# A polysketch attention and feed-forward kernel on one core: the first chunk's preparation laid out and ordered anew

## The chip, the core and the metric

The kernel runs on one core of a Trainium2 chip. The core has a matrix engine (TensorE, PE in the profile, with its weight loads shown apart as PEld), a vector engine (VectorE, DVE), an activation engine (ScalarE, ACT), a general engine (GpSimd, POOL) and a queue engine (SyncE, SP) that issues most transfers. The five run their own instruction streams and wait for one another through semaphores. The metric is the time of the whole kernel on the device in microseconds (us), the median of several runs.

## The reference

Attention with a polynomial sketch in place of the softmax, for 4 batches, 4 heads, 1088 positions and head width 32, and then a feed-forward block of width 128 with a hidden width of 512 on the joined heads.

```python
def phi(x):                                    # r = 8, so 64 features
    a = np.einsum('rd,bhsd->bhsr', S1, x)
    b = np.einsum('rd,bhsd->bhsr', S2, x)
    return np.einsum('bhsi,bhsj->bhsij', a, b).reshape(*x.shape[:-1], r * r)
q_p, k_p = phi(q), phi(k)
kv = np.einsum('bhsf,bhsd->bhfd', k_p, v)
z = np.sum(k_p, axis=2)
attn = np.einsum('bhsf,bhfd->bhsd', q_p, kv) / (np.einsum('bhsf,bhf->bhs', q_p, z)[..., None] + 1e-06)
x = attn.transpose(0, 2, 1, 3).reshape(B, S, H * D)
xn = (x - mean(x)) / np.sqrt(var(x) + 1e-06) * g_ln
out = x + np.maximum(xn @ w_ch1, 0.0) @ w_ch2
```

The arrays q, k, v and g_ln are float32. The sketches S1, S2 and the weights w_ch1 (W1), w_ch2 (W2) are float64, and the kernel makes float32 of them itself.

## The kernel before

**Making floats.** A float64 arrives as two 32-bit words. The kernel takes the high word apart on VectorE (`split`: exponent bits in `ex`, mantissa bits in `bits`, a tensor_scalar each), makes the mantissa and the scaled exponent from them, adds the low word, and joins the parts: `floats(2)` gives the mantissa, `floats(3)` the low word, `floats(0)` and `floats(1)` the exponent on ACT (lines 225 to 235), or `exps` the exponent on POOL (237 to 243, two tensor_scalar); `add` (POOL, line 252) adds the low word; `signed` and `last` (VectorE, 184 and 260) put in the sign and exponent. W1 goes through this in two halves of 256 columns, W2 in one piece of 512. The sketches (128 x 64 numbers here, both sketches side by side, each row repeated for 16 groups of partitions) go through it in lines 188 to 202.

**Loads.** SP issues, in order: S2, the keys of batch 0 in two pieces (`kn`), its queries (`qn`), W1, its values in four pieces (`vn`), W2. ACT issues S1 and the vector g. Batch 0's values go on every fourth partition and its keys are turned into every fourth column; the other batches lie in blocks of 32. The loads of batch 1 and the keys of batch 2 are held back by one small copy on POOL (line 608) that writes into their first column after a piece of the features of the queries is there.

**Attention, batch by batch.** Keys are turned in 32 x 32 blocks by VectorE (`turn_k`, into `kT`), multiplied with the sketch (`key_features`, into `fs`), and multiplied pairwise into 64 features (`key_products`, on POOL and VectorE, into `kp`). `key_sums` and `key_scale` give the denominators' part that is put beside the sketch in `sq`; `key_values` and `key_spread` give the table `kvr`. Queries are turned (`turn_q`, into `qT`), multiplied with `sq` (`query_features`, PSUM tile X), turned back (`query_rows`, into `fq`), divided (`quotients`), multiplied pairwise (`query_products`) and turned (`query_turn`, into `qpT`). `numerators` multiplies `kvr` and `qpT`; `columns_of` copies the result to `xT`.

**Feed-forward, chunk by chunk.** A chunk is 512 rows; a batch gives two, and a last small one holds what is left of all four. `mean_free` multiplies W1 with a matrix that takes out the mean and holds g (`cg`), in two halves. `hidden` does one of four column blocks of W1 and the relu, `second` the product with W2 for 128 rows, `finish` scales and adds x. `turn_rows`, `stats` and `root` make the rows and their scales.

**Order.** Every engine runs its instructions in the order in which the kernel's text issues them; the order is written out by hand, lines 583 to 728 for batches 0 and 1, a loop from line 732 for the rest. `fill` issues matmuls of ones into a bank that nobody reads. What must be waited for is found from the tiles that instructions read and write. The first chunk is half prepared apart from the rest: `(0, 0, 4)` in the order means batch 0's first four of eight tiles of 32 columns.

Of the kernel before, what the change touches and what calls it, by code (L numbers as in the profile page):

```python
# [8 lines left out]
F32 = mybir.dt.float32  # L9
# [16 lines left out]
def kernel(  # L26
# [43 lines left out]
    XP = M[2]  # L70
# [6 lines left out]
    s_raw = const([P, 2 * D], S1.dtype, "s_raw")  # L77
    for eng, src, a in ((act, S1, 0), (nc.sync, S2, D)):
        eng.dma_start(out=s_raw[:, a : a + D],
                      in_=bass.AP(src.tensor, src.offset, [[0, P // R], [D, R], [1, D]]))  # L80
# [7 lines left out]
    act.dma_start(out=g_row, in_=moe_g_ln.rearrange("(o p) -> o p", o=1))  # L88
# [15 lines left out]
    def load_v(b):  # L104
        base = v.offset + b * H * S * D
        for r in range(4):
            n = SN[r] * D
            nc.sync.dma_start(
                out=_ap(vn[b], *((r, 32) if b == 0 else (32 * r, 32)), 0, [[VH, H], [1, n]],
                        step=4 if b == 0 else 1),  # L110
# [4 lines left out]
    for t in vn:  # L115
# [4 lines left out]
    nc.sync.dma_start(out=w1_raw, in_=moe_w_ch1)  # L120
    load_v(0)
    nc.sync.dma_start(
        out=w2_raw.rearrange("p (jc f) -> p jc f", f=DM),
        in_=moe_w_ch2.rearrange("(jc p) f -> p jc f", p=P),
    )
# [20 lines left out]
    dve.tensor_tensor(out=m8, in0=bit, in1=head, op=ALU.is_equal)  # L146
    kT = [const([P, NT * P], F32, f"kT{i}") for i in range(2)]
# [40 lines left out]
    s_f = const([P, 2 * D], F32, "s_f")  # L188
    if s_raw.dtype == F32:
        dve.tensor_copy(out=s_f, in_=s_raw)  # L190
    else:
        t = exponent(s_raw, P, 2 * D, "s")
# [10 lines left out]

    w1 = const([P, DH], F32, "w1")
# [5 lines left out]
    class weight:  # L210


        def __init__(self, dst, raw, tag):
            self.dst, self.raw, self.plain = dst, raw, raw.dtype == F32
            if not self.plain:
                self.t = exponent(raw, P, raw.shape[-1], tag)

        def cols(self, a, n):
            return {k: x[:, a : a + n] for k, x in self.t.items()}
# [17 lines left out]
        def exps(self, a=0, n=512):  # L237
            if not self.plain:
                t = self.cols(a, n)
                pool.tensor_scalar(out=t["exf"], in0=t["ex"], scalar1=-896.0, scalar2=0.0,  # L240
                                   op0=ALU.add, op1=ALU.max)
                pool.tensor_scalar(out=t["e2"], in0=t["exf"], scalar1=255.0, scalar2=2.0**23,
                                   op0=ALU.min, op1=ALU.mult)
# [18 lines left out]
    W1, W2 = weight(w1g, w1_raw, "w1"), weight(w2, w2_raw, "w2")  # L262


    def turn_k(b, r2):
        n = SN[r2]
        at, dims = (r2, [[1, 2], [P, n], [4, 32]]) if b == 0 else (
# [583 lines left out]
```

## Time and profile before

| what | value |
|---|---|
| median of 3 runs | 110.47 us (110.25 to 110.83) |
| the profiled execution: its time, its span | 110.73 us, 108.9 us |
| PE matmul busy | 100.2 us, 92% of the span |
| DVE, POOL, ACT busy | 70.9, 53.9, 39.2 us |
| moved by DMA | 14.19 MB, mean 130 GB/s |
| q of batch 0: issued, landed after | 2.78 us, 5.8 us |
| W1: issued, landed after | 3.26 us, 6.7 us |
| W2: issued, landed after | 6.39 us, 6.5 us |
| batch 1's loads: first issue | 13.67 us |
| first product of the feed-forward block | 19.31 us |

Times inside the profile count from the span's start. A busy PE is not PE at its peak, since matmuls are pipelined; a slice digit is a tenth of busy time. In a timeline row, "x4" is four instructions merged, and the bracket holds the time for which the engine stood idle before the row with the event that ended it. All that is changed runs in the first 26 us.

### The profile page before, as it was taken

The page shows a single profiled execution, that of the slowest core. Times are in us where ns is not written, and L with a number is a line of the kernel's source. Part 1 is how long each engine was busy: PE and PEld are TensorE (multiplying, and loading weights), DVE is VectorE, ACT ScalarE, POOL GpSimd, SP SyncE. Part 2 cuts the span into 40 slices and gives each one's busy share as a digit, 9 for nine tenths or more (in the row PEclk, how much of TensorE's full clock was granted, in tenths as well). Part 3 has the DMA queues.
Part 4 walks back from the last instruction along what each step waited for, and adds up shares of the span by engine and source line. Part 5 has one row for each costly group of instructions (what it writes and reads, how often), then busy time and mean ns, then how long its engine had stood idle before and what let it go on. Part 6 is the DMA issues. An engine that isn't in the chain of part 4 may idle for free. (4 is left out here: it accounts for less than half of the span.)

```text
span 108.9 us, 3605 instructions
## 1 busy us (share of the span) xinstructions
PE 100.2 (92%) x1496; PEld 67.3 (62%) x1496; DVE 70.9 (65%) x204; ACT 39.2 (36%) x79; POOL 53.9 (49%) x67
## 2 busy tenths in 40 slices
PE   6949996994999999999999999999999999999890
PEld 3317545445973677836963786559449658849680
DVE  5496989349859958789879703896950493274411
ACT  4103693662222532434316511451282251071220
POOL 7036682992997397672960693059340034016000
PEclk9999999999999999999999999999999999999998
DMA  1999159910002595334495862520036450132031
GB/s 24 251 332 360 62 174 341 264 45 3 6 0 102 155 303 149 143 106 124 82 355 181 204 211 76 152 56 17 3 76 219 122 163 11 48 91 53 0 96 48
DMA packets 12162, 14.19 MB, mean 130 GB/s; under 512 B 2417, under 2 KB 8946, under 8 KB 12146
## 3 DMA queue, kind: packets, MB, share of 16 engines
q1 hardware_dynamic: 11856, 13.87, 42.8%
q8 instruction: 11, 0.18, 0.7%
q10 hardware_dynamic: 290, 0.10, 0.3%
q14 instruction: 5, 0.04, 0.1%
HBM read 9.77 MB, written 4.19 MB: 128 GB/s over the span
## 5 line engine op out<-in xcount | busy, mean ns | idle before, releaser
L552 PEld LDWEIGHTS M<-w,hT 128*128 128x128 f32 x256 | 31.0, 191 | 7.7 <-issue 3.8
L552 PE MATMUL M<-w,hT 128*128 128x128 f32 x256 | 34.3, 281 | 1.5 <-DVE w L260 1.4
L542 PE MATMUL M<-xT,w 128*128 128x512 f32 (+1 forms) x72 | 34.2, 588 | 0.7 <-DVE ob L564 0.5
L544 ACT ACTIVATE hT<-M 128x512 f32<-128x512 f32 (+1 forms) x36 | 20.6, 574 | 33.7 <-PE M L542 33.7
L432 POOL TENSOR_TENSOR qp<-a,fq 128x1024 f32<-128x1024 f32 (+1 forms) x9 | 16.2, 1816 | 20.0 <-DVE a L425 20.0
L564 DVE SCALAR_TENSOR_TENSOR ob<-M,rstd,x 128x128 f32<-128x128 f32 x32 | 9.0, 344 | 16.5 <-PE M L552 7.1
L542 PEld LDWEIGHTS M<-xT,w 128*128 128x128 f32 x72 | 11.9, 189 | 9.9 <-issue 6.6
L330 POOL TENSOR_TENSOR kp<-fs 128x1024 f32<-128x1024 f32 (+2 forms) x8 | 16.2, 2036 | 2.2 <-ACT fs L324 1.4
L443 DVE STREAM_TRANSPOSE qpT<-qp 128x1024 f32<-128x1024 f32 (+1 forms) x10 | 10.8, 1082 | 4.0 <-POOL qp L432 3.9
L164 PE MATMUL M<-ones 128*128 128x512 f32 (+2 forms) x22 | 10.5, 591 | 1.1 <-DVE ones L86 1.1
L524 POOL TENSOR_SCALAR va<-mv 128x4 f32<-128x4 f32 (+1 forms) x9 | 2.1, 229 | 15.8 <-DVE mv L517 15.6
L526 POOL TENSOR_TENSOR rstd<-va,mhalf 128x4 f32<-128x4 f32 (+1 forms) x9 | 9.0, 1000 | 0.7
L461 PE MATMUL X<-qpT,kvr 32*32 32x256 f32 (+2 forms) x384 | 7.5, 323 | 1.0 <-DVE qpT L443 1.0
L515 DVE BATCH_NORM_STATS2 st<-x 128x6 f32<-128x128 f32 x34 | 7.4, 279 | 0.3
L461 PEld LDWEIGHTS X<-qpT,kvr 32*32 32x32 f32 x384 | 4.5, 103 | 4.4 <-ACT loww L235 1.8
L269 DVE STREAM_TRANSPOSE kT<-kn 128x576 f32<-128x576 f32 (+1 forms) x8 | 6.4, 822 | 1.0 <-DMA kn<-in_k_dram 1.0
L476 ACT COPY xT<-X 128x512 f32<-128x512 f32 (+1 forms) x8 | 4.2, 561 | 7.7 <-PE X L461 7.7
L164 PEld LDWEIGHTS M<-ones 128*128 128x128 f32 x22 | 4.4, 226 | 4.1 <-issue 2.7
L409 DVE STREAM_TRANSPOSE fq<-X 128x512 f32<-128x512 f32 (+1 forms) x9 | 5.8, 669 | 1.0 <-PE X L399 1.0
L507 DVE STREAM_TRANSPOSE x<-xx 128x512 f32<-128x512 f32 (+1 forms) x8 | 5.4, 669 | 0.8 <-DMA xx<-xd 0.8
L358 PEld LDWEIGHTS FB<-kp,vn 128*32 128x32 f32 x288 | 4.2, 110 | 2.6 <-POOL kp L330 1.5
L387 DVE STREAM_TRANSPOSE qT<-qn 128x1024 f32<-128x1024 f32 (+1 forms) x5 | 5.1, 1015 | 0.6 <-DMA qn<-in_q_dram 0.6
(100 smaller groups left out, 85.5 us busy)
## 6 DMA issues: line engine op xcount, KB each, us to landing
qn<-in_q_dram SPq DMA_DIRECT2D x4, 544.0 KB, 5.5
out_dram<-ob SPq DMA_DIRECT2D x33, 64.0 KB, 1.8
xd<-xT SPq DMA_DIRECT2D x7, 256.0 KB, 2.6
xx<-xd SPq DMA_DIRECT2D x28, 64.0 KB, 2.0
kn<-in_k_dram SPq DMA_DIRECT2D x3, 544.0 KB, 6.3
vn<-in_v_dram SPq DMA_DIRECT2D x8, 144.0 KB, 5.1
w_raw<-in_moe_w_ch_dram SPq DMA_DIRECT2D x2, 512.0 KB, 6.6
vn<-in_v_dram SPq DMA_DIRECT2D x8, 128.0 KB, 5.8
```

Source lines behind the costliest of these rows:

```text
L164: pe.matmul(bank[:, 0:w], ones, _ap(ones, 0, P, 0, [[0, w // P], [1, P]]), start=True, stop=True)
L269: dve.transpose(_ap(kT[b % 2], 0, P, at, dims), _ap(kn[b], 0, P, D * ST[r2], [[D * n, 2], [D, n], [1, D]]),)
L330: eng.tensor_tensor(out=_ap(o, 0, P, H * F * t0, [[F, (t1 - t0) * H], [R, R], [1, R]]), in0=_ap(a, 0, P, at, [[R, (t1 - t0) * H], [1, R], ...
L432: eng.tensor_tensor(out=_ap(qp[p, t0 // 4], 0, P, H * F * (t0 % 4), [[F, m], [R, R], [1, R]]), in0=_ap(a2s[p], 0, P, HR * t0, [[R, m], [1, ...
L443: dve.transpose(_ap(qpT[p], 0, P, 32 * t0, [[32, n], [width(p), 8], [1, 32]]), qp[p, t0 // 4][:, o : o + n * H * F],)
L461: pe.matmul(X[D * h : D * h + D, 512 * r + 32 * t0 : 512 * r + 32 * (t0 + n)], kvr[p if p < 4 else r][rows, DM * i + D * h : DM * i + D * ...
L515: dve.bn_stats(out=st[:, 6 * t : 6 * t + 6], in_=x[c][:, P * t : P * (t + 1)])
L526: pool.tensor_tensor(out=rs[:, 0:n], in0=va[:, 0:n], in1=mhalf[:, 0:n], op=ALU.pow)
L542: pe.matmul(hp[:, 0:n], w1[:, P * j : P * (j + 1)], xT[c][:, 0:n], start=True, stop=True)
L544: act.activation(_ap(hT[c], 0, P, 512 * j, dims), hp[:, 0:n], AF.Relu)
L552: pe.matmul(po[c][:, DM * t : DM * (t + 1)], hT[c][:, 512 * j + P * t : 512 * j + P * (t + 1)], w2[:, DM * j : DM * (j + 1)], start=(j == ...
L564: dve.scalar_tensor_tensor(out=ob[c][:, P * t : P * (t + 1)], in0=po[c][:, P * t : P * (t + 1)], scalar=rstd[c][:, t : t + 1], in1=x[c][:, ...
```

## The change

- The sketches are loaded on every fourth partition, S1 on partitions 0, 4, 8, ..., S2 on 1, 5, 9, ..., into a 128 x 32 tile that POOL clears first. After one transpose both lie in one 32-column tile. For the copy of S2 spread over heads (`sketches2`), a matmul with a 0/1 matrix `pick` (from an iota on POOL and a comparison on VectorE) brings its rows to all groups in PSUM.
- Batch 0's keys and values have the same layout as the other batches; `turn_k` can do a range of tiles, and batch 0's keys are turned in four pieces, after the sketches.
- g, W1 and W2 are issued by ACT, after its step for the sketches' mantissa.
- W1's first half is split into PSUM (bank M[0]), its second half later into SBUF.
- W2's exponents are computed by VectorE instead of POOL.
- `kn[1]`'s first column, which holds back the loads of batch 1, is written by ACT from the quotients' result, after `key_spread`.
- The order up to chunk 0's third hidden product is new; the fills go to X, and there are fewer of them. The copy of W1's first finished half moves from ACT to VectorE; the clearing of a part of kT[0] is gone.

```diff
--- before.py
+++ after.py
@@ -67,17 +67,18 @@
 
     X = ps.tile([P, 2048], F32, name="X")
     M = [ps.tile([P, 512], F32, name=f"M{i}") for i in range(3)]
-    XP = M[2]
     FB = ps.tile([P, 512], F32, name="FB")
 
     def const(shape, dtype, name):
         return consts.tile(shape, dtype, name=name)
 
 
-    s_raw = const([P, 2 * D], S1.dtype, "s_raw")
-    for eng, src, a in ((act, S1, 0), (nc.sync, S2, D)):
-        eng.dma_start(out=s_raw[:, a : a + D],
-                      in_=bass.AP(src.tensor, src.offset, [[0, P // R], [D, R], [1, D]]))
+
+    s_raw = const([P, D], S1.dtype, "s_raw")
+    pool.memset(s_raw.bitcast(U32), 0)
+    for eng, src, a in ((act, S1, 0), (nc.sync, S2, 1)):
+        eng.dma_start(out=_ap(s_raw, a, H * R, 0, [[1, D]], step=4),
+                      in_=bass.AP(src.tensor, src.offset, [[0, H], [D, R], [1, D]]))
     one = const([P, 1], F32, "one")
     dve.memset(one, 1.0)
     warm = const([P, 1], F32, "warm")
@@ -85,7 +86,6 @@
     ones = const([P, P], F32, "ones")
     dve.memset(ones, 1.0)
     g_row = const([1, P], moe_g_ln.dtype, "g_row")
-    act.dma_start(out=g_row, in_=moe_g_ln.rearrange("(o p) -> o p", o=1))
     kn = [const([P, G * D], F32, f"kn{b}") for b in range(B - 1)]
     kn.append(kn[0])
     qn = [const([P, G * D], F32, f"qn{b}") for b in range(B)]
@@ -106,8 +106,7 @@
         for r in range(4):
             n = SN[r] * D
             nc.sync.dma_start(
-                out=_ap(vn[b], *((r, 32) if b == 0 else (32 * r, 32)), 0, [[VH, H], [1, n]],
-                        step=4 if b == 0 else 1),
+                out=_ap(vn[b], 32 * r, 32, 0, [[VH, H], [1, n]]),
                 in_=bass.AP(v.tensor, base + ST[r] * D, [[G * D, 32], [S * D, H], [1, n]]),
             )
 
@@ -117,12 +116,7 @@
     load_rows(kn, k, 0, 0, 18)
     load_rows(kn, k, 0, 18, G)
     load_rows(qn, q, 0)
-    nc.sync.dma_start(out=w1_raw, in_=moe_w_ch1)
     load_v(0)
-    nc.sync.dma_start(
-        out=w2_raw.rearrange("p (jc f) -> p jc f", f=DM),
-        in_=moe_w_ch2.rearrange("(jc p) f -> p jc f", p=P),
-    )
 
 
     top = const([P, 1], F32, "top")
@@ -144,6 +138,9 @@
     dve.tensor_scalar(out=bit, in0=row, scalar1=3, scalar2=3,
                       op0=ALU.logical_shift_right, op1=ALU.bitwise_and)
     dve.tensor_tensor(out=m8, in0=bit, in1=head, op=ALU.is_equal)
+    pick = const([P, P], F32, "pick")
+    away = const([P, P], I32, "away")
+    pool.iota(away, [[0, P // R], [4, R]], base=1, channel_multiplier=-1)
     kT = [const([P, NT * P], F32, f"kT{i}") for i in range(2)]
     for t in kT:
         pool.memset(t[:, 8 * P :], 0.0)
@@ -185,11 +182,11 @@
                                  op0=ALU.bitwise_and, op1=ALU.bitwise_or)
 
 
-    s_f = const([P, 2 * D], F32, "s_f")
+    s_f = const([P, D], F32, "s_f")
     if s_raw.dtype == F32:
         dve.tensor_copy(out=s_f, in_=s_raw)
     else:
-        t = exponent(s_raw, P, 2 * D, "s")
+        t = exponent(s_raw, P, D, "s")
         split(t)
         act.activation(t["mant"], t["bits"], AF.Identity, bias=one, scale=2.0**-20)
         dve.tensor_scalar(out=t["exf"], in0=t["ex"], scalar1=-896.0, scalar2=0.0,
@@ -201,6 +198,13 @@
                                  op0=ALU.mult, op1=ALU.add)
         dve.tensor_tensor(out=s_f, in0=t["mant"], in1=t["e3"].bitcast(F32), op=ALU.mult)
 
+    act.dma_start(out=g_row, in_=moe_g_ln.rearrange("(o p) -> o p", o=1))
+    act.dma_start(out=w1_raw, in_=moe_w_ch1)
+    act.dma_start(
+        out=w2_raw.rearrange("p (jc f) -> p jc f", f=DM),
+        in_=moe_w_ch2.rearrange("(jc p) f -> p jc f", p=P),
+    )
+
     w1 = const([P, DH], F32, "w1")
     w2 = const([P, JC * DM], F32, "w2")
     w1g = const([P, DH], F32, "w1g")
@@ -210,13 +214,19 @@
     class weight:
 
 
-        def __init__(self, dst, raw, tag):
+        def __init__(self, dst, raw, tag, bank=None):
             self.dst, self.raw, self.plain = dst, raw, raw.dtype == F32
+            self.bank = bank
             if not self.plain:
                 self.t = exponent(raw, P, raw.shape[-1], tag)
 
         def cols(self, a, n):
-            return {k: x[:, a : a + n] for k, x in self.t.items()}
+            t = {k: x[:, a : a + n] for k, x in self.t.items()}
+            if self.bank is not None and a == 0:
+
+                y = self.bank.bitcast(U32)
+                t["ex"], t["bits"] = y[:, 0:n], y[:, n : 2 * n]
+            return t
 
         def split(self, a=0, n=512):
             if not self.plain:
@@ -237,10 +247,10 @@
         def exps(self, a=0, n=512):
             if not self.plain:
                 t = self.cols(a, n)
-                pool.tensor_scalar(out=t["exf"], in0=t["ex"], scalar1=-896.0, scalar2=0.0,
-                                   op0=ALU.add, op1=ALU.max)
-                pool.tensor_scalar(out=t["e2"], in0=t["exf"], scalar1=255.0, scalar2=2.0**23,
-                                   op0=ALU.min, op1=ALU.mult)
+                dve.tensor_scalar(out=t["exf"], in0=t["ex"], scalar1=-896.0, scalar2=0.0,
+                                  op0=ALU.add, op1=ALU.max)
+                dve.tensor_scalar(out=t["e2"], in0=t["exf"], scalar1=255.0, scalar2=2.0**23,
+                                  op0=ALU.min, op1=ALU.mult)
 
         def signed(self, a=0, n=512):
             if not self.plain:
@@ -259,16 +269,15 @@
                 t = self.cols(a, n)
                 eng.tensor_tensor(out=dst, in0=t["mant"], in1=t["e3"].bitcast(F32), op=ALU.mult)
 
-    W1, W2 = weight(w1g, w1_raw, "w1"), weight(w2, w2_raw, "w2")
-
-
-    def turn_k(b, r2):
-        n = SN[r2]
-        at, dims = (r2, [[1, 2], [P, n], [4, 32]]) if b == 0 else (
-            32 * r2, [[32, 2], [P, n], [1, 32]])
+    W1 = weight(w1g, w1_raw, "w1", bank=M[0])
+    W2 = weight(w2, w2_raw, "w2")
+
+
+    def turn_k(b, r2, t0=0, t1=NT):
+        n = min(t1, SN[r2]) - t0
         dve.transpose(
-            _ap(kT[b % 2], 0, P, at, dims),
-            _ap(kn[b], 0, P, D * ST[r2], [[D * n, 2], [D, n], [1, D]]),
+            _ap(kT[b % 2], 0, P, 32 * r2 + P * t0, [[32, 2], [P, n], [1, 32]]),
+            _ap(kn[b], 0, P, D * (ST[r2] + t0), [[D * SN[r2], 2], [D, n], [1, D]]),
         )
 
     HR, W = H * R, H * R2
@@ -278,23 +287,25 @@
 
     def sketches():
 
-        s_t = const([P, W], F32, "s_t")
+        s_t = const([P, 32], F32, "s_t")
         dve.transpose(s_t, s_f)
         dve.tensor_tensor(
             out=_ap(sk, 0, P, 0, [[HR, 2], [R, H], [1, R]]),
-            in0=_ap(s_t, 0, P, 0, [[HR, 2], [R, H], [1, R]]),
+            in0=_ap(s_t, 0, P, 0, [[1, 2], [0, H], [4, R]]),
             in1=_ap(m32, 0, P, 0, [[0, 2], [1, H], [0, R]]),
             op=ALU.mult,
         )
         for b in range(B):
             pool.tensor_copy(out=_ap(sq[b], 0, P, 0, [[R, 2], [1, R]]),
-                             in_=_ap(s_t, 0, P, 0, [[HR, 2], [1, R]]))
+                             in_=_ap(s_t, 0, P, 0, [[1, 2], [4, R]]))
+        dve.tensor_scalar(out=pick, in0=away, scalar1=0, scalar2=None, op0=ALU.is_equal)
 
     def sketches2():
 
+        pe.matmul(FB[:, P : P + D], pick, s_f, start=True, stop=True)
         dve.tensor_tensor(
             out=_ap(s2b, 0, P, 0, [[D, H], [1, D]]),
-            in0=_ap(s_f, 0, P, D, [[0, H], [1, D]]),
+            in0=_ap(FB, 0, P, P, [[0, H], [1, D]]),
             in1=_ap(m8, 0, P, 0, [[1, H], [0, D]]),
             op=ALU.mult,
         )
@@ -580,84 +591,84 @@
     def mean_free(a, bank):
         pe.matmul(bank[:, 0:half], cg, w1g[:, a : a + half], start=True, stop=True)
 
-    fill(2, XP, 512)
-    turn_k(0, 0)
+    fill(2, X, 512)
     sketches()
-    turn_k(0, 2)
-    fill(1, XP, 512)
+    turn_k(0, 0, 0, 4)
+    turn_k(0, 2, 0, 4)
+    turn_k(0, 0, 4)
+    turn_k(0, 2, 4)
+    fill(1, X, 256)
+    key_features(0, 0, 4, M[0])
+    key_products(pool, 0, 0, 4)
+    key_features(0, 4, 9, M[1])
+    turn_q(0, 0, 4)
     pe.matmul(FB[:, 64:65], g_row, one[0:1], start=True, stop=True)
+    sketches2()
     act.copy(g_col, FB[:, 64:65])
-    pool.tensor_scalar(out=cg, in0=ident, scalar1=-1.0 / DM, scalar2=g_col,
-                       op0=ALU.add, op1=ALU.mult)
-    sketches2()
-    key_features(0, 0, 4, M[0])
-    key_features(0, 4, 9, M[1])
-    key_products(pool, 0, 0, 4)
-    turn_q(0, 0, 4)
-    fill(1, XP, 256)
+    fill(1, X)
     key_sums(0, FB, 0)
-    fill(1, XP)
+    fill(1, X)
     key_scale(0, FB, 32)
     key_products(pool, 0, 4, 6)
     key_products(dve, 0, 6, 9, M[1], 4)
-    fill(1, XP)
+    W1.split(0, half)
+    fill(1, X)
     query_features(0, 0, 4)
-    W1.split()
+    W1.floats(3, 0, half)
     query_rows(0, 0, 4)
-
-    pool.tensor_copy(out=kn[1][:, 0:1], in_=fq[0][:, 0:1])
+    for step in (2, 0, 1):
+        W1.floats(step, 0, half)
+    pool.tensor_scalar(out=cg, in0=ident, scalar1=-1.0 / DM, scalar2=g_col,
+                       op0=ALU.add, op1=ALU.mult)
+    quotients(0, 0, 4)
+    key_values(0)
+    key_rows()
+    W1.floats(3, half, half)
+    fill(1, X, 256)
+    key_spread(0, M[1], 0)
+
+    act.copy(kn[1][:, 0:1], a2s[0][:, 0:1])
     load_rows(kn, k, 1)
     load_rows(qn, q, 1)
     load_v(1)
     load_rows(kn, k, 2)
-    W1.floats(3)
-    W1.floats(2, 0, half)
-    W1.add(0, half)
-    W1.floats(0, 0, half)
-    W1.floats(1, 0, half)
-    W1.floats(0, half, half)
-    quotients(0, 0, 4)
-    fill(1, XP, 512)
-    fill(1, XP, 256)
-    key_values(0)
-    key_rows()
-    W1.floats(1, half, half)
-    fill(1, XP, 256)
-    key_spread(0, M[0], 0)
     query_products(0, pool, 2, 2)
     query_products(0, dve, 0, 2)
     query_turn(0, 0, 2)
     query_turn(0, 2, 2)
+    W1.add(0, half)
     W1.signed(0, half)
     W1.last(dve, 0, half)
-    W1.floats(2, half, half)
-    W1.add(half, half)
+    W1.split(half, half)
     W2.floats(3)
-    fill(1, XP, 512)
+    fill(1, X, 512)
+    fill(1, X, 256)
     numerators(0, 0, 4)
     columns_of(0)
+    for step in (0, 1, 2):
+        W1.floats(step, half, half)
     mean_free(0, M[0])
-    act.copy(w1[:, 0:half], M[0][:, 0:half])
+    dve.tensor_copy(out=w1[:, 0:half], in_=M[0][:, 0:half])
+    turn_q(0, 4, 4)
+    W1.add(half, half)
+    W2.split()
     W1.signed(half, half)
     W1.last(dve, half, half)
-    W2.split()
     W2.exps()
-    turn_q(0, 4, 4)
+    fill(1, M[2])
+
+
+    hidden(0, 0)
     W2.floats(2)
-    fill(1, XP)
-
-
-    pool.memset(kT[0][:, 8 * P + 64 :], 0.0)
-    hidden(0, 0)
     W2.add()
-    mean_free(half, FB)
-    act.copy(w1[:, half:], FB[:, 0:half])
     query_features(0, 4, 4)
     hidden(0, 1)
     W2.signed()
     query_rows(0, 4, 4)
     turn_k(1, 0)
     W2.last(dve)
+    mean_free(half, FB)
+    act.copy(w1[:, half:], FB[:, 0:half])
     turn_rows(0)
     hidden(0, 2)
     quotients(0, 4, 4)
```

## The prediction

> **What bounds the kernel now.** I read the page's busy table and slices first, then the list of waits, then the order of instructions in time from 0 to 32 us, where all the edits lie. The slices put TensorE (PE) near 9 tenths almost everywhere except at the start; the digit of the tenth slice (24.5 to 27.2 us) holds a real gap.
>
> ```profile
> PE   6949996994999999999999999999999999999890
> POOL 7036682992997397672960693059340034016000
> DMA  1999159910002595334495862520036450132031
> ```
>
> After about 26 us PE hardly rests, so time taken out of the start should come out of the end, and time put in should stay in. The chain that ended last covers only the final 6 us and says nothing of the start; so I follow the start's two visible stalls in the order of time. Columns are start, duration, engine, line, operation, and in brackets the idle time before it with its releaser.
>
> ```profile
> 8.63 0.71 DVE L387 STREAM_TRANSPOSE qT<-qn 128x512 f32<-128x512 f32 x1 [0.57 <-DMA qn<-in_q_dram]
> 9.19 3.17 POOL L330 TENSOR_TENSOR kp<-fs 128x1024 f32<-128x1024 f32 x2 [1.36 <-ACT fs L324]
> 9.77 0.96 DVE L330 TENSOR_TENSOR kp<-M,fs 128x768 f32<-128x768 f32 x1 [0.43 <-ACT fs L324]
> 10.65 0.78 DVE L178 TENSOR_SCALAR exw<-w_raw 128x512 uint32<-128x512 uint32 x1
> 11.34 1.30 DVE L180 TENSOR_SCALAR bitsw<-w_raw 128x512 uint32<-128x512 uint32 x1
> 12.56 0.70 DVE L409 STREAM_TRANSPOSE fq<-X 128x512 f32<-128x512 f32 x1
> 14.69 1.58 POOL L432 TENSOR_TENSOR qp<-a,fq 128x512 f32<-128x512 f32 x1 [0.36 <-DVE a L425]
> 16.31 0.71 DVE L443 STREAM_TRANSPOSE qpT<-qp 128x512 f32<-128x512 f32 x1 [0.22 <-POOL qp L432]
> ...
> 18.57 0.42 DVE L178 TENSOR_SCALAR exw<-w_raw 128x512 uint32<-128x512 uint32 x1
> 18.90 0.42 DVE L180 TENSOR_SCALAR bitsw<-w_raw 128x512 uint32<-128x512 uint32 x1
> ```
>
> VectorE (DVE) is the thread here: it waits for q of batch 0, and its two splits of W1 take 0.78 and 1.30 us, though the same shapes take 0.42 each at 18.57, where POOL is idle. POOL's two key products end near 11.15 (9.19 plus 1.96 for the 1024-wide form) and at 12.36 (9.19 + 3.17), and the two splits end just after these instants, 11.43 and 12.64: each got through only when a POOL product had ended. I call the end of the second product transpose T: 16.31 + 0.71 = 17.02. The numerators, the first hidden product (19.31) and all that follows hang on it.
>
> ```profile
> 19.07 2.05 POOL L240 TENSOR_SCALAR exfw<-exw 128x512 f32<-128x512 uint32 x1 [2.12 <-DVE exw L178]
> 21.20 1.94 POOL L242 TENSOR_SCALAR e2w<-exfw 128x512 uint32<-128x512 f32 x1
> 23.18 0.69 DVE L184 SCALAR_TENSOR_TENSOR e3w<-w_raw,e2w 128x512 uint32<-128x512 uint32 x1 [3.24 <-POOL e2w L242]
> 23.31 1.69 POOL L252 TENSOR_TENSOR mantw<-mantw,loww 128x512 f32<-128x512 f32 x1
> 25.09 0.65 DVE L260 TENSOR_TENSOR w<-mantw,e3w 128x512 f32<-128x512 f32 x1
> 25.88 2.02 PE L552 MATMUL M<-w,hT 128*128 128x128 f32 x16 [1.36 <-DVE w L260]
> ```
>
> Second stall: W2's exponents hold POOL 4 us, DVE idles 3.24 us, and PE stands 1.36 us before the second product at 25.88, which is T + 8.86. The question is how far that instant moves.
>
> **Start, to q's transpose.** The new memset of s_raw (about 0.1 to 0.2 us, from POOL's 128-wide memsets at 0.21) goes ahead of both sketch loads, and on SP's queue ahead of k and q: 0 to 0.2 us later; the sketch loads are a quarter as large, which may give that back. Keys: the two transposes with stride took 1.20 and 1.07; the plain forms took 0.73 (24.43) and 0.70 (26.80). In four pieces, with about 0.15 fixed each (0.70 for 512 columns, 1.25 for 1024), that is 1.43 + 2 x 0.15 = 1.75. They begin at 5.44, or at 6.0 for the later half of k (issued 2.31, landed in 3.7), so key features can start near 6.9 rather than 8.00. This removes the 0.43 us wait for fs at 9.77, but not the wait for q, so alone it buys no more than 0.43. Iota, the pick mask and its matmul lie under the wait for q; the copy of S2 now reads PSUM after that wait and costs DVE 0.27 (row L295).
>
> The queue: g, W1 and W2 are issued by ACT after its s mantissa (3.47 + 0.35), near 3.9, 4.6 and 5.3 at 0.65 to 0.72 each; ACT is otherwise idle until its first fs copy, so the issue is free. In the kernel before, W1 stands behind q on SP; now it runs beside q. q landed at 8.58. Lower bound of the delay 0, upper 1.5 (512 KB of W1 at the 350 GB/s of those slices all passing ahead of q's last pieces). I take 0, since q was issued near 2.8, about 2 us ahead of W1.
> The Trainium skill, DMA: Bandwidth & Descriptors, section "Issuing engines are not separate DMA queues", says that transfers from different engines share the same 16 DMA engines and interleave, which speaks against any gain from ACT's queue and for a later q; by the rule alone q would be up to that upper bound later and the sum 0.8 slower than before instead of 0.7 faster, and no run here shows two queues side by side yet.
> v of batch 0 gets 0.4 us earlier in issue and loses some bandwidth; key values need it only near 11 to 12.9, with slack.
>
> **From q to T.** DVE's order becomes: query transpose 0.71, S2 0.27, key product 0.96, half split of W1 into PSUM, feature transpose 0.70, quotients 1.31 (13.30 to 14.61), POOL's query product 1.66 (14.61 to 16.27), last transpose 0.75 (16.27 to 17.02). No row has DVE write such a split to PSUM. Bounds for two 256-wide pieces: 0.4 (half of two free 0.42 rows) and 2.08 (if they still queue behind POOL). I take 0.7: 256 columns at the 0.96 us per 768 of the key product, which touches PSUM and ran freely beside POOL. Sum 0.71 + 0.27 + 0.96 + 0.70 + 0.70 + 1.31 + 1.66 + 0.75 = 7.06 against 17.02 - 8.63 = 8.39: T comes 1.33 earlier. At the upper bound, which is the case that PSUM does not do what it is named for, the sum is 8.44, nothing is gained here, and the whole change is about 0.7 slower (111.2); against it stands the key product at 9.77, with one operand in PSUM, unhindered at 0.96.
>
> ACT's W1 steps (0.37 to 0.51 each) fall between; the three of the first half end by about 13, before kvr needs ACT. Fills removed before key values were 1.56 us of PE from 11.63; nothing then waited for key values but kvr (15.68), so no gain. The first-half mean_free keeps its place: numerators, then 0.70, then a copy of 0.37, now on DVE; hidden stays at T + 2.29.
>
> **From T to the second product.** DVE: W1's first half 0.85 under the numerators, half split, copy (to T + 2.24), query transpose 0.70, W2's splits 0.75, giving T + 3.6 with overlaps. POOL's add of W1's second half waits for ACT's three steps after the xT copy, T + 1.83 + 1.51 = T + 3.34. It takes 0.73. DVE's signed and last (0.85) follow; then POOL's W2 add, which took 1.69 including some 0.56 under DVE's L184 (23.31 to 23.87), so 1.13 alone. DVE's new exponents: two 512-wide, 0.75 as the splits; then signed to last 2.56 (23.18 to 25.74). If DVE and POOL exclude one another as at 10.65, both adds lie in DVE's thread: 3.6 + 0.73 + 0.85 + 1.13 + 0.75 + 2.56 = 9.62, less some 0.3 of overlaps at the handovers, plus 0.14 to the matmul: T + 9.5, which is 0.64 worse than 8.86. If they do not, 9.5 - 1.86 = 7.64, and PE's own work (19.31 to 24.51, 5.2, from T + 2.29, plus about 0.4 for the later w1 copy) sets T + 7.9, 0.96 better. I take the first, the nearest rows. POOL's 4 us leave, but were not worth 4: the new owner is the busier engine.
>
> **The gate of batch 1.** Its copy moves to ACT behind kvr, about 14.3 to 15 rather than 13.33, so six loads go up to 1.5 us later on SP, and behind it ACT's W2 low words. k of batch 1 landed in 4 to 8 us and is wanted at 24.43, q at 30.64: covered; without the cover each late us would count in full.
>
> **Sum.** 1.33 - 0.64 = 0.69 earlier. The profiled execution took 110.73 (span 108.9, 1.83 around it): 110.04. The median of the runs, 110.47, is 0.26 lower; from it 109.8.
>
> **Rivals.**
> 1. The locks overlap little (chance 0.22): 1.33 + 0.96 = 2.3 earlier, 108.2. For it: transposes at 23.79 and 24.43 ran normally under POOL's add. Against: the adds become ready during split and exponents, not transposes.
> 2. Slower (0.22): q lands late. Place: the query transpose at 8.63. Price: 1.5 less the 0.69, so 0.8 slower, 111.3. It decides from a start later than 9.3, where no gain is left. For it: the DMA digits are at 9 from 2.7 us wherever q is in flight. Against: q's head start.
> 3. PE runs at its slow rate (0.14): the opening fills shrink from six 512-wide passes (1.07 to 6.23) to four and two narrow ones, near 5.35. In the trace those passes follow 0.86 apart and later ones 0.43. Key sums, key scale and query features hold 0.38 + 0.25 + 0.51 of PE between q and DVE's feature transpose (rows at 9.83, 10.55 and 11.19); doubled, and with the key features late as well, 0.3 to 1 reaches DVE: about 110.4, no change.
> The Trainium skill, TensorE: Matmul & The Clock Gate, Part 1, gives about 3.4 us of activity for full rate, on a free-running window; the trace's 5.2 us of passes at half rate agree with no fixed delay of 3.4 us, and by the page alone 4.3 us of fills would suffice and this rival would fall away.
> The forecast keeps 0.42.
>
> **Numbers.** Half a per cent, 0.55 us, is about what a measurement of this kernel can tell from no change. Faster (below 109.92): 0.27 from the forecast, all of rival 1, 0.05 of rival 3: 0.54. Within: 0.13 + 0.06 + 0.06 = 0.25. Slower: 0.02 + 0.16 + 0.03 = 0.21. The time is 109.8; its own range 109.2 to 110.4. The wider range, 107.9 to 111.2, takes in rival 1 with 0.3 around it and rival 2 up to just short of its full price; about 0.05 is left out below and 0.13 above.
>
> **What would show it.** Splits of W1 at about 0.35 each beside POOL's products; T near 15.7; POOL's W2 add lying inside DVE's exponent stretch, with a DVE exponent row of 1 us or more; second product near 25.2 with PE still waiting for w. Wrong if the query transpose starts after 9.3, if W1's second half holds mean_free, or if the gain at 25 us isn't the gain at the end.

## The result and the profile after

The changed kernel takes 114.06 us (median of 4 runs, 113.58 to 114.55) against 110.65 for the kernel before in the same comparison: a ratio of 1.0321, 95% interval 1.0257 to 1.0385. It is 3% slower where 0.7 us less was forecast. The ratios here leave out executions that took over 1.5% more than the fastest of their kernel, so a ratio can differ a little from that of two medians, and three of the profiles below are of such executions (their times stand beside them).

The profiled execution took 114.02 us, its span is 112.2 us (108.9 before), its mean granted clock 0.966 (0.996). The slices of the page, 2.8 us each:

```profile
PE   6994299898699999999999999999999999999890
POOL 7347052061299567684692198019612025007000
PEclk9999755999999999999999999999999999999998
DMA  0889701996000279152387474440026440122031
```

The gap that PE had in the tenth slice is there as before, now in the eleventh (digit 6). A new hole stands in the fourth and fifth slices (8.4 to 14 us), and the clock line, all nines before, falls to 7, 5, 5 in the fifth to seventh. The timeline of the changed kernel shows what fills these slices (columns as in the prediction):

```profile
8.79 0.71 DVE L398 STREAM_TRANSPOSE qT<-qn 128x512 f32<-128x512 f32 x1 [2.13 <-DMA qn<-in_q_dram]
...
12.45 0.43 DVE L175 TENSOR_SCALAR M<-w_raw 128x256 uint32<-128x256 uint32 x1 [1.90 <-DMA w_raw<-in_moe_w_ch_dram]
12.91 0.43 DVE L177 TENSOR_SCALAR M<-w_raw 128x256 uint32<-128x256 uint32 x1
13.24 0.70 DVE L420 STREAM_TRANSPOSE fq<-X 128x512 f32<-128x512 f32 x1
13.91 2.15 PE L369 MATMUL FB<-kp,vn 128*32 128x64 f32 x72 [2.07 <-DMA vn<-in_v_dram]
...
16.98 0.71 DVE L454 STREAM_TRANSPOSE qpT<-qp 128x512 f32<-128x512 f32 x1 [0.22 <-POOL qp L443]
17.44 2.33 PE L161 MATMUL X<-ones 128*128 128x512 f32 x4
17.68 0.37 ACT L385 COPY kvr<-M 128x256 f32<-128x256 f32 x1 [0.85 <-PE M L384]
19.70 1.07 PE L472 MATMUL X<-qpT,kvr 32*32 32x128 f32 x64
22.00 1.10 PE L553 MATMUL M<-xT,w 128*128 128x512 f32 x2 [0.39 <-DVE w L651]
...
24.42 1.28 POOL L262 TENSOR_TENSOR mantw<-mantw,loww 128x512 f32<-128x512 f32 x1 [0.71 <-ACT mantw L243]
24.44 1.54 DVE L250 TENSOR_SCALAR exfw<-exw 128x512 f32<-128x512 uint32 x1
26.01 0.43 DVE L252 TENSOR_SCALAR e2w<-exfw 128x512 uint32<-128x512 f32 x1
...
29.17 2.02 PE L563 MATMUL M<-w,hT 128*128 128x128 f32 x16 [1.45 <-DVE w L270]
```

The same steps of PE and ACT in the kernel before:

```profile
13.12 1.21 PE L358 MATMUL FB<-kp,vn 128*32 128x64 f32 x72
15.31 0.37 ACT L374 COPY kvr<-M 128x256 f32<-128x256 f32 x1
17.17 1.06 PE L461 MATMUL X<-qpT,kvr 32*32 32x128 f32 x64 [1.04 <-DVE qpT L443]
```

Reading down: q is on time (8.79 against 8.63 before). After its key product DVE has the split of W1 next in its stream and stands 1.90 us on W1's load; the feature transpose behind it starts at 13.24 instead of 12.56. PE waits 2.07 us for batch 0's values. Windows of half a us show the granted clock at 1.00 until 12.0, 0.86 to 12.5, 0.50 from there to 19.0, 0.81 to 19.5. At half clock the key values take 2.15 (1.21 before), and from their start to the end of the copy to `kvr` it is 18.05 - 13.91 = 4.14 (15.68 - 13.12 = 2.56 before). The fill of 768 columns ahead of the numerators takes 2.33 and ends after the data are ready: T is 16.98 + 0.71 = 17.69 and `kvr` is there at 18.05, but the numerators start at 19.70, T + 2.0. Before, they started at 17.17, T + 0.15. From the first hidden product to the second product it is 29.17 - 22.00 = 7.17 (25.88 - 19.31 = 6.57 before). The second product comes 3.29 later than before, and the span is 3.3 longer.

Of the 3.29, 2.53 are there when the numerators start (19.70 against 17.17), and two loads and the clock are in them; 0.60 come between the first hidden product and the second product, where the forecast had 0.64. The windows of 1 us, kernel before and then changed kernel (columns: window, its length, PE busy with its matmuls, granted clock, DMA share, GB/s):

```profile
9.00:10.00 1.00, 1.00 (x29) 1.00 1.06 365
10.00:11.00 1.00, 1.00 (x30) 1.00 1.00 334
11.00:12.00 1.00, 1.00 (x35) 1.00 0.36 119
```

```profile
9.00:10.00 1.00, 0.08 (x8) 1.00 1.09 251
10.00:11.00 1.00, 1.00 (x29) 1.00 1.06 245
11.00:12.00 1.00, 0.83 (x34) 1.00 1.11 196
12.00:13.00 1.00, 0.00 (x0) 0.68 0.87 223
```

The DMA engines are as fully occupied (share about 1) at some 0.7 of the bytes per us (251 against 365, 245 against 334), and a stream that thins out from 11 us on before goes on past 13.

### The profile page after: what moved, and what is told of

The parts are those of the page before. It is cut to its first block, busy times and chain, and to the rows that moved or that the text cites. A ratio compares the mean times of both kernels' runs of the same rounds, so it can differ in the third digit from the quotient of the medians.

```text
span 112.2 us, 3612 instructions
## 1 busy us (share of the span) xinstructions
PE 102.2 (91%) x1496; PEld 69.2 (62%) x1496; DVE 72.2 (64%) x212; ACT 39.3 (35%) x80; POOL 49.5 (44%) x65
## 5 line engine op out<-in xcount | busy, mean ns | idle before, releaser
L555 ACT ACTIVATE hT<-M 128x512 f32<-128x512 f32 (+1 forms) x36 | 20.6, 574 | 33.3 <-PE M L553 33.3
L161 PE MATMUL X<-ones 128*128 128x512 f32 (+2 forms) x18 | 9.6, 662 | 1.1 <-DVE ones L87 1.1
L369 PEld LDWEIGHTS FB<-kp,vn 128*32 128x32 f32 x288 | 5.1, 125 | 4.6 <-issue 3.1
L369 PE MATMUL FB<-kp,vn 128*32 128x64 f32 x288 | 5.8, 243 | 2.1 <-DMA vn<-in_v_dram 2.1
L161 PEld LDWEIGHTS X<-ones 128*128 128x128 f32 x18 | 4.4, 275 | 4.4 <-issue 3.3
L278 DVE STREAM_TRANSPOSE kT<-kn 128x256 f32<-128x256 f32 (+3 forms) x10 | 5.8, 606 | 0.0
```

The costliest lines, as they stand in the source:

```text
L161: pe.matmul(bank[:, 0:w], ones, _ap(ones, 0, P, 0, [[0, w // P], [1, P]]), start=True, stop=True)
L369: pe.matmul(FB[D * h : D * h + D, 64 : 64 + F], vn[b][:, VH * h + D * t : VH * h + D * (t + 1)], kp[b % 2][:, H * F * t + F * h : H * F * ...
L555: act.activation(_ap(hT[c], 0, P, 512 * j, dims), hp[:, 0:n], AF.Relu)
```

## The experiments

Two theories stood at the start. **Layout:** batch 0's values, each load now going to 32 adjacent partitions instead of every fourth of all 128, slow the whole load stream, W1 in it. **Queue:** W1 issued by ACT runs beside q and the values, takes their share, and is itself late. The first three runs undo one, the other, and both.

**Weights back on SP, new layout kept.**

```
     load_rows(qn, q, 0)
+    nc.sync.dma_start(out=w1_raw, in_=moe_w_ch1)
     load_v(0)
+    nc.sync.dma_start(out=w2_raw..., in_=moe_w_ch2...)
...
-    act.dma_start(out=w1_raw, in_=moe_w_ch1)
-    act.dma_start(out=w2_raw..., in_=moe_w_ch2...)
```

> The changed kernel with W1 and W2 issued by SP again, W1 behind q and W2 behind v, all else as changed. Queue theory (W1 is late because it shares the engines with v and W2): W1 is there before DVE wants it at 10.5, the 1.9 us wait of the split goes, T is near 15.8, and the time is about 110 if the clock then holds. Layout theory (values in blocks of 32 partitions are written at some 220 GB/s where the stepped ones were at 350): W1 is early too, but the values still land near 13.5, PE still stands from 11.8 and the clock still drops; about 112.5.

115.11 us, ratio 1.0374 (1.0291 to 1.0457). Taking the queue back wins nothing, so the queue theory, which had about 110 here, falls. The windows stay slow:

```profile
9.00:10.00 1.00, 0.00 (x0) 0.99 1.00 169
10.00:11.00 1.00, 0.47 (x2) 0.50 1.06 193
```

It is also worse than the layout theory had it: q's transpose starts at 10.65 here, and the clock is at half from 10 us. Why q is late in this order was not followed up.

**Batch 0's keys and values on every fourth partition and column again, the rest of the change kept.**

```
-                out=_ap(vn[b], 32 * r, 32, 0, [[VH, H], [1, n]]),
+                out=_ap(vn[b], *((r, 32) if b == 0 else (32 * r, 32)), 0, [[VH, H], [1, n]],
+                        step=4 if b == 0 else 1),
...
+        at, dims = (r2, [[1, 2], [P, n], [4, 32]]) if b == 0 else (
+            32 * r2, [[32, 2], [P, n], [1, 32]])
...
+    pool.memset(kT[0][:, 8 * P + 64 :], 0.0)
```

> The changed kernel with batch 0's keys and values laid out with a step of 4 as before, W1 and W2 still on ACT's queue. Layout theory: 9 to 12.5 us moves at 330 GB/s or more, W1 lands near 11 instead of 12.4 and the values near 12.5, DVE's wait shrinks to 0.5 us or less, about 111.5. Queue theory: W1 still lands at 12 or later and the time stays near 114.

112.41 us, ratio 1.0072 (1.0004 to 1.0141), from 1.0321. The same windows of this kernel:

```profile
9.00:10.00 1.00, 0.00 (x0) 1.00 1.05 370
10.00:11.00 1.00, 0.59 (x20) 0.95 1.04 360
11.00:12.00 1.00, 1.00 (x12) 0.50 0.51 172
```

The full rate is back. The view of the DMA issues (size of one, median us from issue to landing) shows the two loads, changed kernel first and this one second:

```profile
w_raw<-in_moe_w_ch_dram ACTq DMA_DIRECT2D x2, 512.0 KB, 8.9
vn<-in_v_dram SPq DMA_DIRECT2D x2, 128.0 KB, 9.0
```

```profile
w_raw<-in_moe_w_ch_dram ACTq DMA_DIRECT2D x2, 512.0 KB, 7.4
vn<-in_v_dram SPq DMA_DIRECT2D x2, 128.0 KB, 6.9
```

DVE no longer waits for W1, PE no longer waits for the values, and the second product moves from 29.17 to 27.23. But T hardly moves, 17.62 against 17.69:

```profile
13.16 0.72 DVE L423 STREAM_TRANSPOSE fq<-X 128x512 f32<-128x512 f32 x1 [1.34 <-PE X L413]
17.77 1.06 PE L475 MATMUL X<-qpT,kvr 32*32 32x128 f32 x64 [0.78 <-DVE qpT L457]
```

q's transpose starts at 9.27 here (8.79 in the changed kernel), the clock is at 0.50 from 11 to some 14.3 us, and DVE now stands 1.34 us for the query features. What the values' old layout gives back in these two traces lies behind T: the numerators start at T + 0.15 instead of T + 2.0. Still the kernel isn't faster than before. In its two executions at a mean clock of 0.996 and 0.997 it took 111.19 and 111.02; at 0.985 or less it took 111.78 or more.

**Both undone.**

> Both undone: weights on SP, batch 0 with a step of 4. Both theories: W1 there by 10, values by 12.5, no drop of the clock; the prediction's own sum then holds, about 109.8. If it is still over 111.5, neither the queue nor the layout is the main cause and the order itself is.

The two edits above together: 111.76 us, 1.0119 (1.0034 to 1.0203), where 109.8 was expected. T is 17.35, the second product at 26.79, the clock again at half from 11 to 14.4. So a loss is left in the new order itself. By the line that the expectation drew (over 111.5) the order would even be the main cause; by the medians, undoing both takes back 2.3 of the 4.3 us between the forecast and the changed kernel, and 2.0 stay.

**The layout alone, on the kernel before.**

```
-                out=_ap(vn[b], *((r, 32) if b == 0 else (32 * r, 32)), 0, [[VH, H], [1, n]],
-                        step=4 if b == 0 else 1),
+                out=_ap(vn[b], 32 * r, 32, 0, [[VH, H], [1, n]]),
...
-        at, dims = (r2, [[1, 2], [P, n], [4, 32]]) if b == 0 else (
-            32 * r2, [[32, 2], [P, n], [1, 32]])
+        at, dims = 32 * r2, [[32, 2], [P, n], [1, 32]]
```

> The kernel before with one part alone: batch 0's keys and values in blocks of 32 partitions. Layout theory: 8.5 to 12 us moves at 200 to 250 GB/s instead of 350, the values and W2 land 1 to 3 us later, key values wait for them past 13.1 and the time is 111.5 to 113. Rival (only two queues with this layout are slow): the rate stays at 350 GB/s and the time near 110.6, or 0.3 better for the quicker key transposes.

112.97 us, 1.0157 (1.0105 to 1.0208). Its windows:

```profile
8.00:9.00 1.00, 1.00 (x18) 1.00 1.06 151
9.00:10.00 1.00, 1.00 (x30) 1.00 1.07 178
10.00:11.00 1.00, 1.00 (x37) 1.00 1.11 220
```

From 8 to 11 us the kernel before moved 361, 365 and 334 GB/s. The layout by itself takes that to between 0.4 and 0.7 of it, and the kernel is 1.6% slower. Key values start at 13.47 after 1.07 us of waiting for `vn`, and DVE waits 0.56 us for W1. Yet T is 16.36, 0.66 earlier than before: the keys are turned sooner and q landed 4.7 us after its issue instead of 5.8, so that q's transpose starts at 7.46 instead of 8.63. In this trace the time is lost behind T, in the middle of the 64 numerators:

```profile
16.51 0.51 PE L459 MATMUL X<-qpT,kvr 32*32 32x128 f32 x31
18.47 0.58 PE L459 MATMUL X<-qpT,kvr 32*32 32x128 f32 x33 [1.46 <-issue]
```

PE stands 1.46 us there, waiting for nothing that the profile names; the clock is at 0.50 from some 20.6 to 24 us, and the second product starts at 26.73 instead of 25.88. So this run shows that the layout alone lowers the rate of the whole stream and that the kernel is slower with it; that the loss goes through the two waits it does not show, and what held PE stays open. That the values' loads and not the keys' are the slow ones follows from the place: the keys' loads are the same in both kernels, and only their transposes differ.

**The queue alone, on the kernel before.** W1 and W2 are issued by ACT, as in the change; nothing else.

> The kernel before with one part alone: W1 and W2 issued by ACT after the sketches' mantissa. Queue theory: q or W1 lands over 1 us later, 111.5 or more. Layout theory, by which the queue hardly matters: rate near 350 GB/s, W1 there by 10.5, time within 0.5 of 110.6.

110.97 us, 1.0038 (0.9993 to 1.0083), with 355 to 390 GB/s from 8 to 11 us (in a profiled execution of 113.39 us). ACT's queue is about free.

**The fills.** First on the changed kernel:

```
     fill(1, X)
+    fill(1, M[2], 512)
+    fill(1, M[2], 256)
     key_sums(0, FB, 0)
...
+    fill(2, M[2], 512)
     W1.floats(3, 0, half)
```

> The changed kernel with more fills into bank M[2]: 768 columns before key sums and 1024 before key values, where PE stood from 8.5 to 9.9 and from 11.8 to 13.9. Clock theory (the granted clock of 0.50 from 12.1 to 19.3 costs 0.9 in key values and about 1.6 before the numerators): the clock stays at 1.00, numerators start near 17.8 instead of 19.7, about 112.0. Queue or layout theory alone, with the clock a side show: the DVE split still waits for W1 until 12.4 and the time stays within 0.5 of 114.

114.22 us, 1.0217 (1.0099 to 1.0335), an interval that overlaps the changed kernel's. In the profiled execution (117.35 us) q's transpose started only at 11.99, PE stood 3.26 us before the key sums, and the clock fell all the same (0.50 from 13.0 to 19.8). But two of its four executions ran at a mean clock of 1.000 and took 112.47 and 113.73, against 113.58 to 114.55 for the changed kernel, at 0.966 to 0.970. By these two alone a clock that holds is worth some 1 us, and most of the loss stays; no more than that is decided. On the kernel with both undone, where the loads are not in the way:

```
-    fill(1, X, 256)
+    fill(1, X, 512)
     key_features(0, 0, 4, M[0])
...
     fill(1, X)
+    fill(1, M[2], 512)
+    fill(1, M[2], 256)
     key_sums(0, FB, 0)
```

> The kernel with both undone, with longer fills where PE rested: 512 instead of 256 columns before the first keys, and 768 columns into M[2] before key sums. Clock theory (the 0.50 from 11 to 14.2 makes key sums to query features late, and VectorE waits 1.2 for query features): the granted clock stays at 1.00, query features end before the split of W1 does, T is about 16.5 instead of 17.35, and the time about 110.9. Rival (q's landing alone sets T): T and time stay as they were, 111.8.

111.25 us, 1.0054 (1.0021 to 1.0086); the mean clock goes from 0.984 to 1.000, T from 17.35 to 16.70, the second product from 26.79 to 26.24. The two intervals overlap, so the 0.5 us between the medians is not certain by itself, and of the 0.65 in T, 0.38 is not the fills' doing: q's transpose starts at 8.79 here and at 9.17 in the kernel with both undone, though no load was changed. From q's transpose to T it is 7.91 against 8.18, so the traces give the held clock 0.27; DVE's wait for the query features goes from 1.18 to 0.90. What is left of it shows in this kernel's timeline:

```profile
10.15 0.38 PE L354 MATMUL FB<-fs 128*32 128x32 f32 x18
11.56 0.51 PE L412 MATMUL X<-qT,sq 32*32 32x128 f32 x32
12.24 0.72 DVE L422 STREAM_TRANSPOSE fq<-X 128x512 f32<-128x512 f32 x1 [0.90 <-PE X L412]
```

DVE waits 0.90 us for the query features; these wait for the key scale, and this for the key sums, which start at 10.15. In the kernel with both undone, the same key sums stood 1.02 us with the releaser "ACT g_col", a step that has nothing to do with keys: ACT's copy of g comes out of bank FB, and so does DVE's reading of the spread S2, which has to wait for q's transpose. Three things wait in a row because they share a bank.

**S2 through another bank, and the fill between key sums and key scale.**

```
-        pe.matmul(FB[:, P : P + D], pick, s_f, start=True, stop=True)
+        pe.matmul(M[2][:, 0:D], pick, s_f, start=True, stop=True)
...
-            in0=_ap(FB, 0, P, P, [[0, H], [1, D]]),
+            in0=_ap(M[2], 0, P, 0, [[0, H], [1, D]]),
...
-    fill(1, M[2], 512)
-    fill(1, M[2], 256)
     key_sums(0, FB, 0)
-    fill(1, X)
+    fill(1, X, 512)
     key_scale(0, FB, 32)
```

> The kernel with both undone and longer fills (e6), with S2's spread copy going through bank M[2] instead of FB, and the fill between key sums and key scale. Bank theory (in the changed order key sums wait for ACT's copy of g, and that for VectorE's read of S2 from the same bank FB, after q; key sums started 1.4 after q's transpose did): key sums start before 9.3, query features end before W1's split, VectorE's 0.9 us wait before the feature transpose goes, T is near 15.9 instead of 16.7, and the time about 110.5. Rival (key sums wait for the first key products or for VectorE anyway): T and time as in e6, 111.25.

110.66 us, 1.0016 (0.9983 to 1.0048). ACT's copy of g comes at 8.68, ahead of q's transpose (8.95) and no longer behind S2's reading; key sums start at 9.21 (10.15 before it), DVE waits 0.44 instead of 0.90, T is 16.41, short of the 15.9 expected. Bank and fill were changed together; what is left of DVE's wait is the fill's: key scale has its data by 9.84 (S2's copy, 9.59 + 0.25) and starts at 10.58, behind the fill of 512 columns that PE began at 9.52. The time lies between that of the kernel before it and that of before, with overlapping intervals; the moved wait is what is shown.

**POOL's adds away** (on the kernel with both undone). This kernel leaves out the low words of W1's second half and of W2.

```
     turn_q(0, 4, 4)
-    W1.add(half, half)
     W2.split()
...
     W2.floats(2)
-    W2.add()
     query_features(0, 4, 4)
```

> The kernel with both undone (weights on SP, step of 4), and without POOL's two additions of the low words for W1's second half and for W2; the low words of those are left out of the weights. Lock theory (POOL's two additions of 0.73 and 1.13 stand in VectorE's thread between T and the second product): the second product comes at about T + 8.0 instead of T + 9.4, and the time is some 1.3 under that kernel's 111.8, about 110.4. Rival (VectorE's own added work sets that stretch and the additions lie beside it): T + 9.1 or more and 111.5.

109.86 us, 0.9913 (0.9868 to 0.9958). Timelines, with both adds first and without them second (an execution of 110.32 us):

```profile
22.21 1.56 POOL L262 TENSOR_TENSOR mantw<-mantw,loww 128x512 f32<-128x512 f32 x1 [0.63 <-ACT mantw L243]
22.22 0.42 DVE L250 TENSOR_SCALAR exfw<-exw 128x512 f32<-128x512 uint32 x1
22.68 1.37 DVE L252 TENSOR_SCALAR e2w<-exfw 128x512 uint32<-128x512 f32 x1
...
26.79 2.02 PE L565 MATMUL M<-w,hT 128*128 128x128 f32 x16 [1.29 <-DVE w L270]
```

```profile
21.70 0.42 DVE L250 TENSOR_SCALAR exfw<-exw 128x512 f32<-128x512 uint32 x1
22.15 0.43 DVE L252 TENSOR_SCALAR e2w<-exfw 128x512 uint32<-128x512 f32 x1
...
25.31 2.08 PE L565 MATMUL M<-w,hT 128*128 128x128 f32 x16
```

T is 17.35 in both. The second product starts at T + 9.44 with the adds and at T + 7.96 without: DVE's exponent waits out POOL's add, then PE waits out DVE (1.29 us); without the add nothing holds it.

**The add of W2 behind DVE's exponents, under two transposes** (on the kernel with S2 in another bank).

```
     hidden(0, 0)
-    W2.floats(2)
-    W2.add()
     query_features(0, 4, 4)
...
-    W2.last(dve)
     mean_free(half, FB)
     act.copy(w1[:, half:], FB[:, 0:half])
+    W2.floats(2)
+    W2.add()
+    W2.last(dve)
```

> e9 with ACT's mantissa of W2, and so POOL's addition for W2, one step later, after the copy of W1's second finished half; nothing else moves. Lock theory: the addition then falls beside VectorE's two transposes instead of between its exponents, both exponents take 0.42, the second product comes at about T + 8.4 instead of T + 9.5, and the time is about 109.4, 1% under the kernel before. Rival (the stretch is as long whatever the place of the addition): the second product stays at T + 9.5 and the time equals that of e9.

110.76 us, 0.9989 (0.9947 to 1.0031); the second product at T + 8.96 instead of T + 9.43:

```profile
21.98 0.43 DVE L252 TENSOR_SCALAR e2w<-exfw 128x512 uint32<-128x512 f32 x1
23.04 0.71 DVE L422 STREAM_TRANSPOSE fq<-X 128x512 f32<-128x512 f32 x1
23.46 1.27 POOL L262 TENSOR_TENSOR mantw<-mantw,loww 128x512 f32<-128x512 f32 x1 [2.58 <-ACT mantw L243]
24.77 0.69 DVE L270 TENSOR_TENSOR w<-mantw,e3w 128x512 f32<-128x512 f32 x1 [0.36 <-POOL mantw L262]
25.61 2.02 PE L565 MATMUL M<-w,hT 128*128 128x128 f32 x16 [0.81 <-DVE w L270]
```

Beside the transposes the add costs DVE nothing. T + 8.4 and 109.4 us were expected; the add now comes so late that DVE waits 0.36 us for it, and the time can't be told from that of the kernel before this edit (1.0016). q came late in this profiled execution (9.73), so T is 16.65.

**And the weights on ACT's queue.** The kernel just shown, with W1 and W2 issued by ACT after g, as in the change.

> e10 with W1 and W2 on ACT's queue, as in the change. Layout theory, by which the queue hardly matters: within 0.5 of e10. Queue theory: q, W1 or the values land later, VectorE or PE waits for them, and the time is 1 or more over e10.

110.26 us, 0.9962 (0.9931 to 0.9993); T 16.17, second product at 25.13. This is the change without its layout, with its clock, its bank and its add mended: 0.4% below the kernel before, by an interval that ends just short of 1.

## Why the prediction was wrong, and where it held

**The step that failed** is "v of batch 0 ... loses some bandwidth; key values need it only near 11 to 12.9, with slack". It gave the lost bandwidth no price, and the slack was not there: key values started at 13.91, a full us past that range, after 2.07 us of waiting for `vn`. And it asked only what the values' own lateness does. The loss was some 100 GB/s for all that was in flight (365 to 251 at 9 us), W1 too. I had priced a late q, which never came in the changed kernel, and not a late W1, although DVE's order puts the W1 split ahead of the feature transpose. The trace before held the clue: batch 1's values already went to blocks of 32 partitions, and where they were in flight, 19.5 to 20.5 us, it shows 222 and 233 GB/s at a share of 1.15, against 365 at 9 us. That the layout costs time is shown both ways, undone in the changed kernel (1.0321 to 1.0072) and put alone into the kernel before (1.0157).

The Trainium skill, SBUF — State Buffer, section "Door 1: The DMA port swizzle (why `[64,N]` ≈ `[32,N]`)", says that 32 adjacent partitions reach only 8 of the 16 ports, and that the rate goes with the ports that one transfer reaches. The windows agree, 151 to 220 GB/s with the blocks and 334 to 365 without. That section speaks of one transfer alone; that W1, on all partitions, is slowed with it is what these runs add.

By the terms of the sum, second product forecast at 15.69 + 9.5 = 25.19, measured at 29.17, 3.98 later:

| term | forecast | measured | difference |
|---|---|---|---|
| q's transpose | 8.63 | 8.79 | +0.16 |
| DVE waits for W1 | 0 | 1.90 | +1.90 |
| rest of q to T | 7.06 | 8.90 - 1.90 = 7.00 | -0.06 |
| T to the first hidden product | 2.29 | 22.00 - 17.69 = 4.31 | +2.02 |
| hidden to second product | 9.5 - 2.29 = 7.21 | 7.17 | -0.04 |

109.8 + 3.98 = 113.8 against 114.06: nearly all of the miss is two terms. They are what stood on the path in this execution. They are not prices of the two causes: with the old layout back, W1's 1.90 was gone and T still gained only 0.07, since q came 0.48 later and 1.34 of waiting for the query features took the place of W1's; the 1.94 gained at the second product came out of the other term.

**The second failed term**, T to hidden, was taken over from before; it is the late values and the clock together. "Fills removed before key values ...; nothing then waited ...; so no gain" looked at those fills as work only. In the changed kernel PE stands from about 8.5 to 9.9 and from 11.84 to 13.91, the second time for the values, and the clock halves. Of the 2.02, the runs isolate little: with full-rate loads, holding the clock by more fills was worth 0.27 us from q to T, and in the changed kernel some 1 us by two executions. How the 2.02 divide is read from the timeline: `kvr` came 0.36 after T, and the rest is a fill of 2.33 that held the numerators; the same fill took 1.46 at full clock, with the weights back on SP. No run shows the clock's part in the changed kernel by itself, since the one meant to came out undecided. Rival 3 named the clock and priced it at no change, at the query features; it came at the key values and the numerators, with another price.

**The queue**: "I take 0" was right in the changed kernel and on the kernel before (1.0038, 0.9993 to 1.0083). Rival 2 had the right kind of mishap, a load that lands late, on the wrong tile. The skill's rule on issuing engines, weighed there against ACT's queue, foretold no gain; its later q did not show.

**q to T**: with the two waits out of it the sum of 7.06 holds: 7.00 in the changed kernel less its wait, 6.92 where nothing waited (the add behind the exponents). The split into PSUM took 0.43 for each piece (0.35 assumed, far from the upper bound of 2.08 for the two). That bound was hardly put to the test: in the changed kernel POOL was idle by then, from 10.52 to 15.38. Where POOL did work beside it, to 11.27 in the kernel with S2 in another bank, the pieces at 10.62 and 11.07 took 0.41 and 0.43. What the sum missed is the bank that g, S2 and the key sums share: in the kernel with the clock held DVE waits 0.90 us for the query features, and another bank, with a fill moved, took that to 0.44; in the changed kernel it lay hidden under the wait for W1. One slip ahead of q changes nothing: 1.43 + 2 x 0.15 is 1.73, not 1.75.

**T to the second product**: the choice that DVE and POOL exclude one another, T + 9.5, was right: T + 9.61, 9.44, 9.54 and 9.43 in the four kernels with the new order and full-rate loads, T + 7.96 without the adds where T + 7.9 was worked out. The sign named for it, an exponent row of DVE of 1 us or more, is there (1.54 in the changed kernel). Rival 1, little overlap of the locks, falls with it.

**From there to the end**: "time taken out of the start should come out of the end" held within half a us. The second product's shift and that of the span, against before: +3.29 and +3.3 for the change, +1.35 and +1.5 for the layout undone, -0.57 and -0.4 without adds, -0.75 and -0.7 for the last kernel; only the kernel with the weights back on SP lost 1.3 more later.

**Batch 1's gate** was to be up to 1.5 us later; its first load was issued at 18.17 instead of 13.67, since the copy sits behind `kvr`. Still nothing up to 30 us waited for it, so the cover named there held.

What stays open: why q and g were late with the weights back on SP; how much of the layout's loss the values' loads alone would give without the keys' quicker transposes, which were only changed together; what held PE among the numerators when the layout was changed alone; and why q landed anywhere from 5.2 us after its issue (the queue alone) to 6.9 (the add behind the exponents) in kernels whose loads ran at the full rate. That spread is larger than the gains of the last small edits, so one trace of each can't rank them.

## What to carry to other kernels

A load that has slack by its own due time can lose it, and can set the pace of every load beside it: price a changed destination layout by GB/s at full share, and look for the same layout elsewhere in the trace. When a step is moved forward in an engine's stream, ask when its own operand lands, since all behind it waits too. Fills are worth keeping until the work that replaces them is really there, and no longer: one can itself hold the step behind it. Scratch banks are worth sharing only among steps that become ready together.

## What was not expected of the hardware

- Loads to 32 adjacent partitions kept the DMA engines' share at 1.0 or above while the whole stream fell from 334 to 365 GB/s down to 151 to 220; the share alone looks like full speed.
- Two rests of PE, some 1.4 and 2.1 us with 2 us of work between them, were followed by nearly 7 us at a granted clock of 0.50 (12.4 to 19.2), five of them with PE busy. The Trainium skill, TensorE: Matmul & The Clock Gate, Part 1, speaks of an idle window of about 3.4 us; neither rest was as long.
- POOL's add took its turn between two back-to-back operations of DVE: 0.42 for the first exponent, 1.37 for the second; beside transposes it ran in 1.27 and they in their usual 0.71 and 0.73.
